# Another order for the head of a convolution and maxout kernel: 38 tiny matmuls for the band, blocks 0 and 1 mixed

## The chip, the core and the metric

The kernel runs on one core of a Trainium2 chip. The engines are TensorE (PE, matmuls; weight loads are shown apart as PEld), VectorE (DVE), ScalarE (ACT), GpSimd (POOL) and SyncE (SP, which only issues transfers here). Each works through its own instructions in order; they wait for each other with semaphores. The metric is the device time of one execution in microseconds; lower is better. Before the change the median of 11 runs is 482.29 us (481.16 to 484.39).

## The reference

x is 8 sequences of 4160 positions of 192 numbers. A causal convolution of 7 taps mixes each position with the six before it; the taps are a softmax over `weight`, one row per head, and a head is 24 neighbouring channels. What comes out is 33280 tokens of 192, and each goes through a maxout layer: three products of 192 by 768, of which the largest element is kept, and one product back to 192.

```python
w = softmax(weight)                                  # 8 heads x 7 taps
y[s, h*24:h*24+24] = sum(w[h, k] * x[s - 6 + k, h*24:h*24+24] for k in range(7))
hid = np.maximum(np.maximum(y @ w1, y @ w2), y @ w3)  # 33280 x 768
out = hid @ w_out                                    # 33280 x 192
```

## The kernel before

The tokens are cut into 65 blocks of 512 (the last is made of the 8 sequence ends). The kernel holds to the order in which it is written: each engine does its instructions as they stand in the code.

*The maxout.* max(a, b, c) is c + max(0, ...) in a form for which only differences are needed: `wd` holds w1 - w3 in partitions 0 to 63 and w2 - w3 in partitions 64 to 127 (`make_wd`, L252), so `copy_w3` (L256) first puts w3 beside w2. `l1(t, j)` (L374) computes the j-th of six groups of 128 hidden units of block t, the "product" of this document: two halves of TensorE (`lp` and `lq`, three passes each) read `yd`, the block after the convolution, which therefore lies twice, in partitions 0 to 63 and 64 to 127. ScalarE takes the relu of `lp` (L387), VectorE the maximum of that and `lq` (L388). `lp` and `lq` come from pools of two PSUM buffers each (`psp`, `psq`), so a product needs the buffers of the one two before it. `st2(t, u)` (L390) is a sixth of the second layer of block t; it also multiplies `yd` with `m16`, the product of w3 and w_out, which carries the part c. `make_m` (L296) makes m16 from `w3t` (w3 transposed by `transpose_w3`, L278) and `wo`.

*The convolution* is a matmul with a band matrix: `band` holds, for each head, the taps along a diagonal, 32 columns and 6 more at a time. It is built at the start (L211 to L268): the exponentials of the taps, spread over 128 partitions by a matmul, seven shifted copies made by VectorE (`shifted`), summed by seven matmuls with an identity (`band_sum`), and four ScalarE copies into place. From block 2 on, `conv(t)` (L312) convolves each head in 32 columns of TensorE, `evac` copies the two PSUM tiles to `ys`, `repack` (L359) moves six pieces by DMA, issued by SP and POOL in turn, into channel order in `yd`, and `double` (L369), a DMA of SP, copies the lower half of `yd` to the upper. Blocks 0 and 1 don't take this way: `conv_dense` (L331) computes all 192 channels dense, in three PSUM banks, each with the 64 channels in both halves, 120 matmuls a block, and evicts them straight into `yd`; the input for it is `xz` (`cast_dense`, L154).

*Inputs.* SP issues x0, the weights, x1, w_out and x2 to x5 one behind the other; ScalarE issues the taps and a part of w2. `cast_x` (L138) is POOL's.

*The head before.* The dense convolution of block 0, products (0,0) to (0,3), the transposes, the dense convolution of block 1, conv 2, products (0,4) and (0,5) with the m products and conv 3 around them. Then the loop (L493): for each t a product of block t and a sixth of the second layer of block t-1 by turns, with the convolutions of later blocks (three blocks ahead, two at a time in even t) after the first product.

*The end.* Block 63's output is one store of POOL; block 64's goes out in four, by SP and ScalarE.

`keep_warm` puts in matmuls on zeros.

Of the kernel before, what the change touches and what calls it, by code (L numbers as in the profile page):

```python
# [14 lines left out]
P = 128  # L15
# [12 lines left out]
def kernel(  # L28
# [58 lines left out]
    xfp = ctx.enter_context(tc.tile_pool(name="xfp", bufs=6))  # L87
# [11 lines left out]
    NDENSE, AHEAD = 2, 3  # L99
# [11 lines left out]
    def load_x(t):  # L111
# [9 lines left out]
        while i < n:  # L121
# [8 lines left out]
            nc.sync.dma_start(out=xf[0:rlen, i:k + 1, :], in_=src)  # L130
# [23 lines left out]
    def cast_dense(t, copies):  # L154
        xf, _, parts = xin[t]
        for v, copy in enumerate(copies):
            for s in range(CYC // 32):
                cut = GRP * (32 * s // GRP + 1)
                a, b = (32 * s, cut) if v == 0 else (cut, 32 * s + 32)
                for (rl, q0, q1) in parts:  # L160
                    copy(  # L161
                        out=xz[t][0:rl, q0:q1, v, :].rearrange("p q (k c) -> p q k c", c=CYC)[:, :, :, a:b],
                        in_=xf[0:rl, q0:q1, :].rearrange("p q (k c) -> p q k c", c=CYC)[:, :, :, a:b])


    ws = const.tile([P, NC, DFF], FP32)
    w3s = const.tile([P, NC, DFF], FP32)
    wos = const.tile([P, NJ, D], FP32)

    def load_w(eng, st, lo, wsrc, f0, f1):  # L170
        eng.dma_start(out=st[lo:lo + HALF, :, f0:f1],
                      in_=wsrc.rearrange("(c r) f -> r c f", r=HALF)[:, :, f0:f1])

    FA = 2 * P
    wk = const.tile([1, NHEAD * KW], FP32)
    nc.scalar.dma_start(out=wk[:], in_=bass.AP(tensor=weight.tensor, offset=0,
                                               ap=[[0, 1], [1, NHEAD * KW]]))
    load_x(0)
    load_w(nc.scalar, ws, HALF, moe_w2, 0, FA)
    load_w(nc.sync, w3s, 0, moe_w3, 0, FA)  # L180
    load_w(nc.sync, ws, 0, moe_w1, 0, FA)
    load_w(nc.sync, w3s, HALF, moe_w3, FA, DFF)
    load_w(nc.sync, ws, 0, moe_w1, FA, DFF)
    load_w(nc.sync, ws, HALF, moe_w2, FA, DFF)
    load_x(1)
    nc.sync.dma_start(out=wos[:], in_=moe_w_out.rearrange("(j p) c -> p j c", p=P))
    for t in range(2, 6):
        load_x(t)

    idle = const.tile([P, NBLK], FP16)  # L190
    nc.vector.memset(idle[:], 0.0)
    def keep_warm(n):

        ps = psp.tile([P, NBLK], FP32, tag="p", name="idle")
        for _ in range(n):
            nc.tensor.matmul(ps[:], lhsT=idle[:, 0:P], rhs=idle[:], start=True, stop=True)  # L196
# [10 lines left out]

    unit = const.tile([P, 32 + 2 * PAD], FP16)  # L211
    nc.vector.memset(unit[:], 0.0)  # L212
    with nc.allow_low_precision("ones and zeros"):
        nc.vector.reduce_sum(out=unit[:, PAD:PAD + 32],
                             in_=ident[:].rearrange("p (a c) -> p c a", c=32), axis=AXX)
# [3 lines left out]
    ones = const.tile([1, P], FP32)  # L219
    nc.vector.memset(ones[:], 1.0)  # L220
    keep_warm(2)
    wps = psq.tile([P, NHEAD, KW], FP32, tag="q", name="wps")
    nc.tensor.matmul(wps[:].rearrange("p h k -> p (h k)"), lhsT=ones[:], rhs=wk[:],  # L223
                     start=True, stop=True)
    wexp = const.tile([P, NHEAD, KW], FP32)
    nc.scalar.activation(out=wexp[:], in_=wps[:], func=AF.Exp)
    wsum = const.tile([P, NHEAD], FP32)
    nc.vector.reduce_sum(out=wsum[:], in_=wexp[:], axis=AXX)
    wrec = const.tile([P, NHEAD], FP32)
    nc.vector.reciprocal(out=wrec[:], in_=wsum[:])  # L230
    taps = const.tile([P, NHEAD, KW], FP16)
    nc.vector.tensor_mul(out=taps[:], in0=wexp[:],
                         in1=wrec[:].unsqueeze(2).to_broadcast([P, NHEAD, KW]))
    shifted = const.tile([P, KW, NHEAD, WIN], FP16)
    for k in range(KW):
        one = unit[:, k:k + WIN]
        nc.vector.tensor_mul(out=shifted[:, k, :, :],
                       in0=bass.AP(tensor=one.tensor, offset=one.offset,
                                   ap=[list(one.ap[0]), [0, NHEAD], [1, WIN]]),
                       in1=taps[:, :, k:k + 1].to_broadcast([P, NHEAD, WIN]))  # L240

    keep_warm(7)
    ps = psq.tile([P, NHEAD, WIN], FP32, tag="q", name="band_sum")
    for k in range(KW):
        nc.tensor.matmul(ps[:], lhsT=ident16[:], rhs=shifted[:, k, :, :],  # L245
                         start=(k == 0), stop=(k == KW - 1))
    keep_warm(3)
    w3h = const.tile([P, NC, DFF], FP16)
    parts_w3 = ((0, 0, FA), (HALF, FA, DFF))
    wd = const.tile([P, NC, DFF], FP16)  # L250

# [4 lines left out]
    def copy_w3(copy, part):  # L256
        lo, f0, f1 = part
        copy(out=w3s[HALF - lo:P - lo, :, f0:f1], in_=w3s[lo:lo + HALF, :, f0:f1])

    def cast_w3(copy, part):  # L260
        lo, f0, f1 = part
        copy(out=w3h[lo:lo + HALF, :, f0:f1], in_=w3s[lo:lo + HALF, :, f0:f1])

    cast_dense(0, (nc.scalar.copy, nc.scalar.copy))
    copy_w3(nc.scalar.copy, parts_w3[0])
    make_wd(0, 1)
    for a in range(4):
# [279 lines left out]
```

The softmax here doesn't subtract the row's maximum and nothing guards it: scores larger than these inputs give would overflow.

## Time and profile before

| | |
|---|---|
| median of 11 runs | 482.29 us |
| the profiled execution | 481.91 us |
| its span | 479.9 us |
| TensorE busy | 468.1 us, 98% of the span |
| VectorE, ScalarE, POOL busy | 366.0, 327.2, 211.2 us |
| first dense matmul | 10.75 us |
| first matmul of conv 2 | 20.89 us |
| first product of block 2 | 33.25 us |
| last matmul / last output in SBUF | 473.7 / 474.4 us |

Times in the profile count from the start of the span. A line of the timeline has the start, the duration, the engine, the line of the kernel, and the output and inputs; "x3" are several instructions in one line. A line of the chain of waits has a start, a duration and what the chain stood on: the chain is followed back from the last instruction to what released it. "Granted clock" is the share of TensorE's full clock that it was given. A transfer's issue and its landing are told apart: "to landing" is from one to the other.

### The profile page before, as it was taken

What the parts mean: (1) busy time and instruction counts of PE and PEld (TensorE: products, weight loads), DVE (VectorE), ACT (ScalarE), POOL (GpSimd) and SP (SyncE); (2) the same over time, 40 slices, a digit from 0 to 9 for tenths busy, and PEclk for the clock granted to TensorE, in tenths of its full rate; (3) what the DMA queues carried; (4) which work ended last, traced back from release to release, by engine and by line L of the source; (5) the groups of instructions that cost most, each with busy time, mean ns of one, the idle gap of its engine ahead of it and who ended that gap; (6) DMA issues with size and microseconds to landing.
All of it is one profiled execution on the core that took longest, in us unless ns stands there. A gap on an engine that the chain in (4) does not pass through costs nothing.

```text
span 479.9 us, 21944 instructions
## 1 busy us (share of the span) xinstructions
PE 468.1 (98%) x9083; PEld 393.8 (82%) x9083; DVE 366.0 (76%) x609; ACT 327.2 (68%) x608; POOL 211.2 (44%) x341
## 2 busy tenths in 40 slices
PE   7899999999999999999999999999999999999994
PEld 3478888888888888888888888888888888888994
DVE  6667877778787877877787777778777777778774
ACT  5676667666666767666666766676676767667663
POOL 2654534553454455345435543543545354345210
PEclk9899999999999999999999999999999999999998
DMA  8867756665756666566566656666656656644312
GB/s 190 227 186 213 207 150 193 171 187 159 204 170 168 183 191 172 152 203 181 168 180 181 178 154 195 170 190 168 177 157 192 186 169 186 170 125 135 112 44 95
DMA packets 67603, 82.08 MB, mean 171 GB/s; under 512 B 9424, under 2 KB 55760, under 8 KB 67504
## 3 DMA queue, kind: packets, MB, share of 16 engines
q1 hardware_dynamic: 53934, 49.01, 40.7%
q0 software_dynamic: 13216, 31.38, 18.4%
q8 instruction: 71, 1.16, 1.1%
q10 hardware_dynamic: 354, 0.30, 0.2%
q14 instruction: 28, 0.23, 0.1%
HBM read 30.31 MB, written 25.56 MB: 116 GB/s over the span
## 4 chain that ended last, share of the span: by engine, by line
PE 97%; DVE 1%; ACT 1%; issue 0%; POOL 0%; POOLq 0%
PE lp L383 32%; PE po L426 30%; PE lq L383 26%; PE G L322 7%; PE D L342 1%; PE idle L196 1%; PE band_sum L245 0%; ACT band L268 0%; DVE h L388 0%; ACT r L387 0%; DVE xz L216 0%; PE pm L301 0%; PE wps L223 0%; PE pm L305 0%; DVE band L218 0%
## 5 line engine op out<-in xcount | busy, mean ns | idle before, releaser
L388 DVE TENSOR_TENSOR h<-r,lq 128x512 f16<-128x512 f16 x390 | 267.1, 685 | 102.0 <-ACT r L387 102.0
L387 ACT ACTIVATE r<-lp 128x512 f16<-128x512 f32 x390 | 232.7, 597 | 135.2 <-PE lp L383 90.3
L383 PE MATMUL lp<-yd,wd 64*128 64x512 f16 x1170 | 315.6, 377 | 0.1
L383 PE MATMUL lq<-yd,wd 64*128 64x512 f16 x1170 | 315.1, 375 | 0.0
L426 PE MATMUL po<-wo,h 64*128 64x192 f16 x3120 | 231.7, 243 | 0.0
L426 PEld LDWEIGHTS <-h 64*128 64x128 f16 x3120 | 187.5, 94 | 25.4
L383 PEld LDWEIGHTS <-wd 64*128 64x128 f16 x2340 | 164.4, 94 | 20.9 <-issue 1.8
L452 POOL DMA_DIRECT2D out_dram<-o x64 | 50.7, 792 | 245.7 <-DVE o L436 233.6
L366 POOL DMA_DIRECT2D yd<-ys x189 | 95.4, 509 | 2.1 <-ACT ys L353 1.5
L426 PE MATMUL po<-m,yd 64*128 64x192 f16 x780 | 87.2, 243 | 0.0
L436 DVE TENSOR_TENSOR o<-a,po 128x384 f32<-128x384 f32 (+1 forms) x132 | 71.4, 542 | 0.6 <-ACT a L435 0.6
L146 POOL CAST x<-xf 112x960 f16<-112x960 f32 x62 | 61.7, 995 | 2.9 <-DMA xf<-in_x_dram 2.8
L435 ACT COPY a<-po 128x384 f32<-128x384 f32 (+1 forms) x132 | 61.7, 469 | 1.2 <-PE po L426 1.2
L426 PEld LDWEIGHTS <-yd 64*128 64x128 f16 x780 | 55.2, 94 | 7.9
L322 PEld LDWEIGHTS <-x 112*32 112x32 f16 x2480 | 29.9, 97 | 13.3 <-issue 13.2
L353 DVE CAST ys<-G 128x512 f16<-128x512 f32 x60 | 38.5, 683 | 0.0
L353 ACT CAST ys<-G 128x512 f16<-128x512 f32 x66 | 35.8, 589 | 2.1 <-PE G L322 0.8
L322 PE MATMUL G<-band,x 112*32 112x103 f16 (+1 forms) x2480 | 34.9, 210 | 0.0
L161 POOL CAST xz<-xf 112x240 f16<-112x240 f32 (+2 forms) x6 | 2.4, 438 | 11.0 <-DMA xf<-in_x_dram 11.0
L196 PE MATMUL idle<-idle 128*128 128x512 f16 x14 | 5.9, 561 | 1.2 <-DVE unit L212 1.2
L342 PE MATMUL D<-band,xz 112*32 112x103 f16 (+1 forms) x240 | 3.8, 230 | 0.9 <-ACT band L268 0.9
L342 PEld LDWEIGHTS <-xz 112*32 112x32 f16 x240 | 3.5, 108 | 1.3 <-issue 1.3
(50 smaller groups left out, 41.2 us busy)
## 6 DMA issues: line engine op xcount, KB each, us to landing
out_dram<-o POOLq DMA_DIRECT2D x64, 384.0 KB, 4.2
xf<-in_x_dram SPq DMA_DIRECT2D x57, 420.0 KB, 4.5
yd<-yd SPq DMA_DIRECT2D x63, 192.0 KB, 3.5
yd<-ys SPq DMA_DIRECT2D x63, 48.0 KB, 3.8
yd<-ys POOLq DMA_DIRECT2D x63, 48.0 KB, 3.3
xf<-in_x_dram SPq DMA_DIRECT2D x8, 252.0 KB, 3.3
yd<-ys SPq DMA_DIRECT2D x63, 32.0 KB, 3.3
yd<-ys POOLq DMA_DIRECT2D x63, 32.0 KB, 3.4
```

What stands on the lines that cost most here:

```text
L146: nc.gpsimd.tensor_copy(out=v[0:rl, q0:q1, :], in_=xf[0:rl, q0:q1, :])
L322: nc.tensor.matmul(G[i][32 * g:32 * g + 32, lo:hi], lhsT=x16[0:rlen, cb:cb + 32], rhs=band[0:rlen, h, cc:cc + hi - lo], start=True, stop=T ...
L342: nc.tensor.matmul(ps[32 * g:32 * g + 32, lo:hi], lhsT=xz[t][0:rlen, q, v, 32 * s:32 * s + 32], rhs=band[0:rlen, h, cc:cc + hi - lo], star ...
L353: copy(out=slots[t][:, i, :], in_=convs[t][i][:])
L366: (nc.sync, nc.gpsimd)[n % 2].dma_start(out=yd[r0:r0 + rows, c, :], in_=slots[t][s0:s0 + rows, half, :])
L383: nc.tensor.matmul(ps[i][:, 0:N], lhsT=wd[row, c, P * j:P * (j + 1)], rhs=y[row, c, 0:N], start=(c == 0), stop=(c == NC - 1))
L387: nc.scalar.activation(out=r[:, 0:N], in_=ps[0][:, 0:N], func=AF.Relu)
L388: nc.vector.tensor_max(out=hs[t][:, j, 0:N], in0=r[:, 0:N], in1=ps[1][:, 0:N])
L426: nc.tensor.matmul(ps[b0, i][:, s % 2, :], lhsT=a, rhs=b, start=first, stop=last)
L435: nc.scalar.copy(out=a[:, ss, :], in_=ps[s0, 0][:, ss, :])
L436: nc.vector.tensor_add(out=outs[t][:, s0:s + 1, :], in0=a[:, ss, :], in1=ps[s0, 1][:, ss, :])
L452: qs[i].dma_start(out=bass.AP(tensor=out.tensor, offset=r * D, ap=[[D, n], [step * D, s1 - s0], [1, D]]), in_=ob[p0:p0 + n, s0:s1, :])
```

## The change

The band is built on 8 partitions: taps of a head in one line each, and 38 matmuls, one for each column of the band window, take a shifted piece of that line (8 by 32) against an 8 by 8 identity. The four ScalarE copies into `band` remain. Block 0's casts go from ScalarE to VectorE.

The dense convolution of blocks 0 and 1 computes each channel once, in two PSUM banks (128 channels and 64), 60 matmuls a block; what is evicted lies in one half of `yd`, and VectorE copies it across to the other (`cross`).

Weights are loaded in three parts of 256 hidden units, x1 after the first; w_out, x2 and x3 are issued by ScalarE, between its relus. POOL casts w3, ScalarE evicts all transposes, which now take their PSUM from `psw`.

The head's order is new: products of block 0 and block 1 by turns, then the second layers of both, with conv 2 and conv 3 in between, both in `psp` and `psq`. Block 2 then runs with no second layer beside it, and the convolutions 4 to 6 are placed anew; from block 4 on the loop is the same, but that x is loaded one block later, into five buffers instead of six. Block 0's second layer adds the m products last. Block 63's output is stored in two parts by SP.

```diff
-    xfp = ctx.enter_context(tc.tile_pool(name="xfp", bufs=6))
+    xfp = ctx.enter_context(tc.tile_pool(name="xfp", bufs=5))
...
+    PW = 2 * P
+    def load_w(part):
+        f = slice(PW * part, PW * (part + 1))
+        for st, lo, wsrc in ((w3s, 0, moe_w3), (ws, 0, moe_w1), (ws, HALF, moe_w2)):
+            nc.sync.dma_start(out=st[lo:lo + HALF, :, f],
+                              in_=wsrc.rearrange("(c r) f -> r c f", r=HALF)[:, :, f])
+    wk = const.tile([NHEAD, KW], FP32)
+    nc.scalar.dma_start(out=wk[:], in_=weight)
     load_x(0)
-    load_w(nc.scalar, ws, HALF, moe_w2, 0, FA)
...
+    load_w(0)
     load_x(1)
-    nc.sync.dma_start(out=wos[:], in_=moe_w_out.rearrange("(j p) c -> p j c", p=P))
-    for t in range(2, 6):
-        load_x(t)
+    load_w(1)
+    load_w(2)
...
+    line = const.tile([NHEAD, WIN + 31], FP16)
...
+    keep_warm(6)
+    nc.scalar.activation(out=wexp[:], in_=wk[:], func=AF.Exp, accum_out=wsum[:])
     nc.vector.reciprocal(out=wrec[:], in_=wsum[:])
+    nc.vector.tensor_scalar(out=line[:, 31:31 + KW], in0=wexp[:], scalar1=wrec[:], scalar2=None,
+                            op0=mybir.AluOpType.mult)
+    bps = psq.tile([32, WIN, NHEAD], FP32, tag="q", name="band_cols")
+    for c in range(WIN):
+        nc.tensor.matmul(bps[:, c, :], lhsT=line[:, WIN - 1 - c:WIN + 31 - c],
+                         rhs=ident16[0:NHEAD, 0:NHEAD], start=True, stop=True)
+    keep_warm(4)
+    for a in range(4):
+        nc.scalar.copy(out=band[32 * a:32 * a + 32, :, 32 * a:32 * a + WIN],
+                       in_=bps[:].rearrange("p c h -> p h c"))
+    cast_dense(0, (nc.vector.tensor_copy, nc.vector.tensor_copy))
...
-    for k in range(KW):
-        nc.tensor.matmul(ps[:], lhsT=ident16[:], rhs=shifted[:, k, :, :],
-                         start=(k == 0), stop=(k == KW - 1))
...
+        for n, slots_ in enumerate((range(4), range(4, 6))):
...
+                    for g, s in enumerate(slots_):
...
+            if n == 0:
+                copies[0](out=yd[0:HALF, 0, :], in_=ps[0:HALF, :])
+                copies[1](out=yd[HALF:P, 1, :], in_=ps[HALF:P, :])
+            else:
+                copies[2](out=yd[0:HALF, 2, :], in_=ps[0:HALF, :])
+
+    def cross(t):
+        yd = dense[t]
+        for c in range(NC):
+            a, b = (slice(HALF, P), slice(0, HALF))[::-1 if c == 1 else 1]
+            nc.vector.tensor_copy(out=yd[a, c, :], in_=yd[b, c, :])
...
+    copy_w3(nc.vector.tensor_copy, 0)
+    make_wd(0, 2)
+    conv_dense(0, (nc.scalar.copy, nc.scalar.copy, nc.scalar.copy))
+    cross(0)
+    cast_w3(0)
+    cast_dense(1, (nc.gpsimd.tensor_copy, nc.scalar.copy))
+    cast_w3(1)
+    cast_w3(2)
+    l1(0, 0)
+    nc.scalar.dma_start(out=wos[:], in_=moe_w_out.rearrange("(j p) c -> p j c", p=P))
+    transpose_w3(0)
+    l1(0, 1)
+    load_x(2, nc.scalar)
+    copy_w3(nc.scalar.copy, 1)
+    conv_dense(1, (nc.scalar.copy, nc.vector.tensor_copy, nc.scalar.copy))
+    cross(1)
+    make_wd(2, 4)
+    l1(1, 0)
+    l1(1, 1)
+    copy_w3(nc.scalar.copy, 2)
+    l1(0, 2)
+    transpose_w3(1)
+    l1(0, 3)
+    load_x(3, nc.scalar)
+    nc.gpsimd.tensor_copy(out=wo[:], in_=wos[:])
+    cast_x(2)
+    make_wd(4, 6)
+    l1(1, 2)
+    l1(1, 3)
+    l1(0, 4)
+    transpose_w3(2)
+    l1(0, 5)
+    make_m(0)
+    make_m(1)
+    l1(1, 4)
+    st2(0, 0, NJ)
+    conv(2, PQ)
+    evac(2, 0)
+    evac(2, 1, nc.vector.tensor_copy)
+    repack(2)
+    load_x(4)
+    load_x(5)
+    st2(0, 1, NJ)
+    l1(1, 5)
+    st2(0, 2, NJ)
+    st2(0, 3, NJ)
+    double(2)
+    cast_x(3)
+    conv(3, PQ)
+    evac(3, 0)
+    evac(3, 1, nc.vector.tensor_copy)
+    repack(3)
+    st2(0, 4, NJ)
+    st2(0, 5, NJ)
+    store(0, 0, 4, (nc.gpsimd,))
+    for u in range(NJ):
+        st2(1, u, NJ)
+    cast_x(4)
+    cast_x(5)
+    load_x(6)
+    double(3)
+    store(1, 0, 4, (nc.gpsimd,))
+    loads_at = {2: (7,), 3: (8, 9)}
+    casts_at = {2: (), 3: (7, 8)}
+    convs_at = {2: (4, 5), 3: (6,)}
+    repacks_at = {2: (4,), 3: (5, 6)}
+    doubles_at = {2: (), 3: (4,), 4: (5, 6)}
+    for t in range(2, NB):
+        for u in loads_at.get(t, (t + 6,)):
+            load_x(u)
+        for u in casts_at.get(t, (t + 5,)):
+            cast_x(u)
+        for u in doubles_at.get(t, (t + 2,)):
+            double(u)
         begin(t)
         l1(t, 0)
...
+            if t == NB - 1 and j == 3:
+                store(t - 1, 0, 2, (nc.sync,))
+        if t == NB - 1:
+            store(t - 1, 2, 4, (nc.sync,))
```

## The prediction

> **What bounds the kernel now.** I read the page first (busy times, slices, chain), then the chain of waits and the timeline of the first 42 us, then the granted clock in windows of one us. From the page:
>
> ```profile
> span 479.9 us, 21944 instructions
> PE 468.1 (98%) x9083; PEld 393.8 (82%) x9083; DVE 366.0 (76%) x609; ACT 327.2 (68%) x608; POOL 211.2 (44%) x341
> PE   7899999999999999999999999999999999999994
> PE 97%; DVE 1%; ACT 1%; issue 0%; POOL 0%; POOLq 0%
> ```
>
> TensorE is full in all slices but the first two and the last. From about 26 us on, a step of the loop is one first-layer product and a sixth of a second layer: the next product starts 1.06 us after the last, with no gap (timeline, TensorE):
>
> ```profile
> 29.01 0.38 PE L383 MATMUL lp<-yd,wd 64*128 64x512 f16 x1
> 29.65 0.58 PE L426 MATMUL po<-wo,h 64*128 64x192 f16 x10
> 30.07 0.38 PE L383 MATMUL lp<-yd,wd 64*128 64x512 f16 x1
> ```
>
> So a product costs TensorE 0.64 us (29.01 to 29.65) and a sixth 0.42 (29.65 to 30.07). The change leaves the loop from block 4 on as it is. It can win or lose only in the head and in the last microseconds, and the question is when the same work is behind TensorE. The chain of waits of the head:
>
> ```profile
> 10.75 1.55 PE D L342 x110
> ...
> 13.40 0.59 ACT r L387
> ...
> 14.02 0.70 DVE h L388
> ...
> 14.73 0.37 PE lp L383
> ```
>
> This is the row that matters most. A product with no second layer beside it ends in relu 0.59, then the maximum 0.70, and only then are its two PSUM buffers free for the next but one. A pair of bare products takes 0.43 + 0.38 + 0.59 + 0.70 + hand-overs = 2.2 us, of which TensorE works 1.28. And the head's clock, in windows (last columns: granted clock, DMA share, GB/s):
>
> ```profile
> 16.00:17.00 1.00, 0.26 (x3) 0.00 (x0) 0.50 (x2) 0.97 (x3) 1.00 (x4) 1.00 1.12 298
> 17.00:18.00 1.00, 0.33 (x6) 0.21 (x6) 1.00 (x2) 0.28 (x1) 1.00 (x2) 1.00 1.09 284
> ...
> 20.00:21.00 1.00, 1.00 (x60) 1.00 (x56) 0.69 (x1) 0.17 (x1) 0.52 (x2) 0.50 1.07 285
> 21.00:22.00 1.00, 1.00 (x50) 0.85 (x40) 0.00 (x0) 0.66 (x2) 0.67 (x2) 0.50 0.29 78
> ```
>
> TensorE was busy 0.26 and 0.33 for two windows; then it ran at half clock from 19.8 to about 23.2.
>
> **The change part by part.** I lay the new orders of the engines out with these durations and look for the time at which the second layer of block 2 starts. Before, that is 41.48 us (its first matmul in the timeline, after block 3's first product at 40.83); both kernels have done the same by then, but for the smaller dense convolutions.
>
> *Band.* wk had landed by 3.42, when the wps matmul's releaser ended. Exp 0.22 and its accumulated sum, 0.35 in all; reciprocal 0.20 and multiply 0.22 with hand-overs: 4.2 us. Then 38 tiny matmuls. No row shows one. Lower bound 13 ns (120 dense matmuls in 1.55 us, four side by side, which these are not); upper 67 ns (12 transposes of 64x64 in 0.80 us). I take 55 ns (the other group, 6 in 0.33 us), as they too are small and each loads its own weights: 2.1 us, and 0.2 drain: 6.5. Four band copies at 0.41: 8.2, against 10.75. The four idle matmuls hide beside them, and so do the six casts of block 0 on VectorE (ScalarE's row 1.45 for six, from x0's landing at 5.07). Gain so far 2.5 us; bounds of the tiny matmuls -1.6 and +0.5 on it. The Trainium skill has a lower price: TensorEngine Tiling (Array Packing), Instruction Overhead, gives every matmul about 60 cycles, however few its columns. At the 2.4 GHz of its first page (Trainium Kernel Development and Optimization, NeuronCore Architecture) that is an estimated 1.0 us for the 38, and the sum would be 1.1 us smaller by it; no run here shows it.
>
> *Dense convolution.* Block 0: 10 rounds of four and 10 of two, at 52 ns a round, 1.04 us for 1.55. But two of three evictions went to different engines before; now all three stand on ScalarE (0.58, 0.52 apart), then a crossing copy. A crossing copy's bounds: 0.20 (a sixth of the 64x1536 copy of 1.22) and 0.69 (an eviction of 512 columns); 0.28 taken, nearer to SBUF to SBUF of 16 bit; at 0.69 it adds 1.9 over both blocks. Bank one is done 0.75 after 8.2, the evictions end at 9.6, 10.1, 10.6, the last crossing at 10.95: the third pass of the first product starts there, before at 12.98. The 2.5 has shrunk to 2.0.
>
> *ScalarE's queue.* Behind relu (0,0) at 11.4 stand, in order: w_out's issue 0.52, the transposes' eviction 0.48, relu (0,1) 0.60, x2's issue 0.57, a w3 copy 0.83, and only then block 1's evictions, 14.8 to 15.9. Issues bounded by ScalarE's own two rows (0.52, 0.69) and SP's row of an x load that was stalled, 4.16; I take the short ones, because ScalarE's queue has nothing outstanding then. TensorE has done block 1's convolution by 13.3 and its next product is block 1's: it stands until 15.7, 2.5 us.
>
> *Mixing.* Ten bare products, two groups of transposes (0.33 each), the two m products (1.25): 8.3 us of TensorE work from 15.7. They go in pairs of 2.2, with two differences wd (1.01 each) and m's copies in VectorE's order between the maxima; (1,4) starts at 25.9, the first sixth of block 0's second layer at 26.5, conv 2 at 26.9. Before, conv 2 was at 20.89: seven products, the m products and a sixth more stand ahead of it now, and make it 6.0 later. The transfers that ScalarE issues are hidden: w_out, issued at 11.9, is wanted at 24.2 and x2, issued at 13.4, at 26.9, and even the landings of before (10.7 and 12.9, behind all the weights) would do. x3, issued at 20.2, lands by 24.7 at the loop's 4.5; at 12.9 it would hold conv 3 by some 2 us.
>
> *Block 2's way.* Conv 2 at 26.9, its evictions end at 28.7 (VectorE's behind a maximum), three issues on SP of 0.62, landing 3.5 (medians 3.3 to 3.8): 33.0. Double: 3.6 (3.5 median): 36.7. Behind that wait stand SP's repack 3 and double 3, which then lands near 42, just ahead of block 3. Beside it TensorE has 6.3 us of work for 9.8 us (conv 2, 3: 1.08; five sixths 2.1; product (1,5) 0.64; block 1's second layer 2.52), so it stands 3.4 us: 1.5 ahead of conv 3, whose cast POOL does after repack 2's issues, and 1.9 ahead of block 2. Before, the double of block 2 was issued at 28.92, landed at 32.5, and its product followed at 33.25 without a gap. Bounds: landings of 2.8 and 3.0 give -1.3, of 4.8 (the head's largest) and 4.5 (x4, x5 are ahead in SP's queue) +2.2.
>
> *Block 2 alone.* Its six products have no second layer beside them, as block 1's is done: conv 4, 5 and products are 4.9 us of work in 6.6. Then block 3's first product, conv 6, and block 2's second layer starts at 44.9: 3.4 after 41.48.
>
> *Clock.* The half-clock stage of before is inside the 41.48. The new head has a pause of 2.5 us and then ten us of TensorE busy a little over half, and may get one of its own, bounded by 0 and three stages; in the one seen, block 1's convolution took 2.14 for 1.55, conv 2 0.86 for 0.57 and product (0,4) 1.24 for 0.64: 1.5 us, less what would have been waits. I add 1.0, one stage. The Trainium skill (TensorE: Matmul & The Clock Gate, Why this matters for your kernels) asks for no pauses over about 3 us, and by that rule nothing is added, as no pause of my layout is so long, and the sum is 1.0 less. The trace of before disagrees: its longest pause ahead of the half clock was 1.3 us.
>
> *End.* Block 63's store goes out in two SP parts, the first some 3 us earlier, instead of one POOL store at 472.81 beside the last four; DMA ran at 364 to 190 GB/s until 476.7. Bounds 0 and -0.5: -0.2. Five xf buffers and loads one block later: a load takes 4.5, its cast comes about 6.5 us after the issue; nothing. If that cover went, POOL would wait and with it repack, which has two blocks of 6.97 us to spare.
>
> Sum: 3.4 + 1.0 - 0.2 = +4.2 us. The profiled execution took 481.91 (span 479.9 and 2.0 around it), so 486.1; it lies 0.38 below the median of 482.29, which gives 486.5.
>
> **The rivals.**
> 1. *Half clock for most of the head.* For it: ten us at half load. Against: the old head, 0.93 busy at 12.8 to 16.2, kept full clock. Three stages instead of one: +2.6, 489.1.
> 2. *ScalarE's issues stall as SP's did.* For: SP's x3 took 4.16. Against: that was with eight loads queued ahead on SP. One stall of 3.6 more ahead of block 1's evictions: 490.1.
> 3. *The other side: bare products don't go in pairs of 2.2.* If the two blocks' products overlap so that relu and maximum never hold TensorE, the 2.5 us of waits in the mixing (10.8 us for 8.3) and 1.7 in block 2 go, and the clock stage with them: 486.5 - 4.2 - 1.0 = 481.3. It decides below about 1.5 us a pair. Against: 13.40, 14.02, 14.73 in the chain, and both blocks draw on the same two buffers a side.
> 4. *The unknown terms all at their lower ends:* landings -1.3, tiny matmuls -1.6, no half clock -1.0: 482.6, no measurable change. For it: the tiny matmuls and the landings at a quiet moment are in no row. Against: all three would have to hold.
>
> **How the numbers follow.** Forecast 0.58 (its own range 484 to 488.5); rivals 1 and 2 0.15 and 0.09; rival 3 0.10; rival 4 0.08. About 0.2% is what a measurement of this kernel tells from no change, 481.3 to 483.3. Faster 0.10, within 0.07, slower 0.83. The range leaves out rival 3, and of rival 2 about half and a little of rival 4: 482.5 to 490.
>
> **What would show it.** Band copies end near 8.2; TensorE idle 2 to 3 us before block 1's first product, released by VectorE's crossing copy; that product near 15.7; conv 2 near 27; TensorE idle before block 2's first product, released by the double's DMA; block 2's second layer near 45; then 6.97 us a block as before. I am wrong if the products of blocks 0 and 1 follow each other in much under 1.1 us, or if block 2 is there before block 1's second layer ends.

## The result, and the profile after

The changed kernel takes 485.75 us (median of 13 runs, 483.99 to 488.17), the kernel before 482.44 beside it (50 runs). The ratio is 1.0066, with a 95% interval of 1.0050 to 1.0082: it is slower by 2.4 to 4.0 us. (A ratio leaves out executions that stand far above the others of their kernel, as three of run e10's do below.) The prediction was 486.5, slower by 4.2. Three of its terms were wrong in size, though, and they happen to cancel, so that it came this close is luck in part: this section and the experiments are about those terms.

The page of the changed kernel:

```profile
span 484.3 us, 21755 instructions
PE 468.2 (97%) x8988; PEld 389.8 (81%) x8988; DVE 366.8 (76%) x610; ACT 324.9 (67%) x605; POOL 211.5 (44%) x340
PE   7777999999999999999999999999999999999996
PE 92%; DMA 3%; ACT 1%; DVE 1%; issue 1%; SPq 1%; ACTq 0%
```

TensorE has the same 468 us of work as before and a span 4.4 us longer. It now reads 7 in four slices (48 us) instead of one, and DMA has 3% of the chain where it had none. The last slice reads 6 instead of 4: the end is better. From there on the steady state is what it was, 13.95 us for two blocks in both traces.

The marks of TensorE's timeline, to be held against the times predicted:

```profile
3.87 1.13 PE L225 MATMUL band_cols<-ident,line 8*32 8x8 f16 x38
...
6.72 1.09 PE L307 MATMUL D<-band,xz 112*32 112x103 f16 x60 [0.76 <-ACT band L229]
...
13.31 0.37 PE L358 MATMUL lp<-yd,wd 64*128 64x512 f16 x1 [1.51 <-ACT yd L313]
...
15.16 0.58 PE L358 MATMUL lp<-yd,wd 64*128 64x512 f16 x1 [0.44 <-DVE yd L323]
...
26.99 0.64 PE L288 MATMUL G<-band,x 112*32 112x103 f16 x40
...
31.24 0.64 PE L288 MATMUL G<-band,x 112*32 112x103 f16 x40 [1.58 <-POOL x L146]
...
38.08 0.43 PE L358 MATMUL lq<-yd,wd 64*128 64x512 f16 x1 [2.56 <-DMA yd<-yd]
...
47.59 0.34 PE L402 MATMUL po<-m,yd 64*128 64x192 f16 x3
```

The 38 tiny matmuls take 1.13 us, 30 ns each, and the first dense matmul starts at 6.72, 4.0 us sooner than before. Block 1's first product comes at 13.31 with its second pass at 15.16, so most of the lead is gone by then; conv 2 starts at 26.99, 6.1 us later than before; block 2's first product waits 2.56 us for the transfer that doubles its rows; and block 2's second layer starts at 47.59, where it was at 41.48. That is a head 6.1 us late, of which the end gives 1.6 back.

The chain of waits across the pause ahead of block 2 (start, duration, what):

```profile
29.59 2.92 DMA yd<-ys
...
32.65 5.39 DMA yd<-yd
```

The doubling transfer, issued at 32.65, landed after 5.4 us. And the granted clock, in windows (the last three columns are granted clock, DMA share and GB/s):

```profile
15.00:16.00 1.00, 0.84 (x6) 0.34 (x7) 0.94 (x3) 0.00 (x0) 0.00 (x0) 0.50 1.12 275
16.00:17.00 1.00, 1.00 (x8) 0.49 (x6) 0.58 (x2) 0.60 (x1) 0.00 (x0) 0.50 1.04 206
...
39.00:40.00 1.00, 1.00 (x37) 0.71 (x40) 0.36 (x1) 0.60 (x1) 0.00 (x0) 0.50 1.13 304
40.00:41.00 1.00, 1.00 (x58) 0.98 (x48) 0.33 (x1) 0.59 (x1) 0.00 (x0) 0.50 0.95 322
```

There are two stages of half clock, 14.4 to 17.8 and 38.3 to 41.7, each behind a pause of TensorE; before there was one, 19.6 to 23.0.

### The profile page after: what moved, and what is told of

The parts are those of the page before. It is cut to its first block, busy times and chain, and to the rows that moved or that the text cites. A ratio compares the mean times of both kernels' runs of the same rounds, so it can differ in the third digit from the quotient of the medians.

```text
span 484.3 us, 21755 instructions
## 1 busy us (share of the span) xinstructions
PE 468.2 (97%) x8988; PEld 389.8 (81%) x8988; DVE 366.8 (76%) x610; ACT 324.9 (67%) x605; POOL 211.5 (44%) x340
## 4 chain that ended last, share of the span: by engine, by line
PE 92%; DMA 3%; ACT 1%; DVE 1%; issue 1%; SPq 1%; ACTq 0%
PE lp L358 31%; PE po L402 29%; PE lq L358 26%; PE G L288 7%; DMA xf<-in_x_dram 1%; DMA yd<-yd 1%; ACT r L362 1%; DMA yd<-ys 1%; DVE h L363 1%; SPq L176 0%; ACT w3s L247 0%; DVE yd L323 0%; SPq L130 0%; ACT w3t L260 0%; DVE yd L314 0%
## 5 line engine op out<-in xcount | busy, mean ns | idle before, releaser
L328 DVE CAST ys<-G 128x512 f16<-128x512 f32 x63 | 40.5, 683 | 2.3 <-PE G L288 2.3
L328 ACT CAST ys<-G 128x512 f16<-128x512 f32 x63 | 34.2, 588 | 4.8 <-PE G L288 3.5
L204 PE MATMUL idle<-idle 128*128 128x512 f16 x10 | 3.8, 530 | 1.2 <-DVE idle L199 1.2
L251 POOL CAST w3h<-w3s 64x768 f16<-64x768 f32 x3 | 2.5, 819 | 4.6 <-DMA w3s<-in_moe_w_dram 4.6
L243 DVE TENSOR_TENSOR wd<-ws,w3s 128x768 f16<-128x768 f32 x3 | 2.9, 956 | 0.9 <-DMA ws<-in_moe_w_dram 0.9
L307 PEld LDWEIGHTS <-xz 112*32 112x32 f16 x120 | 2.0, 96 | 1.6 <-DVE xz L163 1.2
```

What stands on the lines that cost most here:

```text
L328: copy(out=slots[t][:, i, :], in_=convs[t][i][:])
```

## The experiments

All times are set against the kernel before, run beside it on the same chip (482.8 to 482.9 there; the changed kernel's +3.2 us is its 0.66%). Because the steady state never changes, one mark sums up a head: the start of convolutions 9 and 10, in block 6, which is at 61.97 in the trace of before and at 68.09 in the changed kernel's.

| run | edit | median, us | ratio to before (95%) | mark, us |
|---|---|---|---|---|
| e1 | before, split last store | 481.21 | 0.9956 (0.9935 to 0.9978) | 62.53 |
| e2 | after, whole last store | 487.02 | 1.0080 (1.0053 to 1.0106) | 66.78 |
| e3 | after, x4 and x5 loaded early | 483.82 | 1.0016 (0.9995 to 1.0038) | 66.58 |
| e4 | after, idle matmuls in two pauses | 485.23 | 1.0040 (1.0016 to 1.0063) | 67.71 |
| e5 | before, tiny band, split store | 485.24 | 1.0045 (1.0029 to 1.0061) | 67.75 |
| e6 | as e5, dense in two banks | 482.18 | 0.9983 (0.9963 to 1.0002) | 63.69 |
| e7 | as e3, block 5 repacked early | 487.01 | 1.0094 (1.0064 to 1.0124) | 70.93 |
| e8 | as e5, VectorE's copy of w3 later | 484.49 | 1.0038 (1.0018 to 1.0058) | 65.89 |
| e9 | as e8, x4 and x5 loaded late | 481.30 | 0.9964 (0.9939 to 0.9989) | 63.40 |
| e10 | as e3, doublings ahead of loads | 487.58 | 1.0082 (1.0056 to 1.0108) | not read |
| e11 | after, more PSUM for bare products | 484.81 | 1.0048 (1.0024 to 1.0071) | 68.04 |
| e12 | e1, x4 and x5 late, idle matmuls | 480.94 | 0.9955 (0.9935 to 0.9975) | 63.28 |

**The end: e1 and e2.** The same edit, put into the one kernel and taken out of the other.

```
 (e1, into the kernel before; e2 takes the same lines out of the changed one)
             st2(t - 1, j, NJ)
-        store(t - 1, 0, 4, (nc.gpsimd,))
+            if t == NB - 1 and j == 3:
+                store(t - 1, 0, 2, (nc.sync,))
+        if t == NB - 1:
+            store(t - 1, 2, 4, (nc.sync,))
+        else:
+            store(t - 1, 0, 4, (nc.gpsimd,))
```

> The kernel before, with one edit: block 63 is stored as the changed kernel does it, in two parts on SyncE, the first after four of the six sixths, instead of one GpSimd store. Read from the two traces: in the changed kernel the end of the span lies 3.9 us after the last sum is in SBUF, against 5.5 before. Theory A (the store of block 63 alone does this, beside the same last four small stores): 1.6 us faster than before, about 480.8. Theory B (the prediction's price, with 0.5 as its bound): 0.2 faster, 482.2. Theory C (the end gains because the changed kernel's last blocks are otherwise laid out, not by the store): no change, 482.4.

> The changed kernel, with block 63 stored again as one GpSimd store behind its six sixths. Theory A: 1.6 us slower than the changed kernel, 487.3. Theory B: 0.2 slower, 485.9. Theory C: no change, 485.7. Together with the run of the kernel before with the split store this says whether the term of the end stands by itself in both kernels.

In the timeline of e1, its span and VectorE's last sum:

```profile
core 0 of [0], span 479.3 us
...
475.01 0.35 DVE L436 TENSOR_TENSOR o<-a,po 128x192 f32<-128x192 f32 x1 [0.17 <-ACT a L435]
```

and in that of the kernel before:

```profile
core 0 of [0], span 479.9 us
...
474.07 0.35 DVE L436 TENSOR_TENSOR o<-a,po 128x192 f32<-128x192 f32 x1 [0.17 <-ACT a L435]
```

From the end of the last sum to the end of the span it is 3.9 us in e1 (479.3 - 475.36) and 5.5 before (479.9 - 474.42); it is 3.9 in the changed kernel and 5.5 in e2 (484.6 - 479.11). So block 63's store alone is worth 1.6 us at the end, in either kernel: theory A. The times agree for e1 (2.1 us faster, 1.1 to 3.1). In e2 the time moved by 0.7 us (1.0080 against 1.0066, intervals that overlap), which by itself shows neither 1.6 nor nothing. Its profiled head is 1.3 shorter than the changed kernel's, for a reason that the next paragraphs need: it had no second half-clock stage. Which part of the store costs (its size, GpSimd's queue, or the later issue) wasn't separated.

**The doubling's landing: e3.**

```
     load_w(2)
+    load_x(4)
+    load_x(5)
...
     repack(2)
-    load_x(4)
-    load_x(5)
```

> The changed kernel, with the loads of x4 and x5 issued on SyncE right behind the last weights instead of behind the repacking of block 2. In the changed kernel's trace the doubling of block 2, issued at 32.7, landed after 5.4 us, where 3.6 was predicted, and block 2's first product waited for it; TensorE stood 2.6 us, and a stage of half clock followed. Theory A (the two loads, issued just ahead in the same queue, hold the doubling): it lands after about 3.6 us, block 2's first product comes near 36.3 instead of 38.1, the pause shrinks to under 1 us and the second half-clock stage goes with it: 2 to 3.5 us faster than the changed kernel, 482.3 to 483.8. Theory B (the landing of 5.4 has another cause, such as the stores or a slow transfer from SBUF to SBUF): it stays above 5 us and the time within 0.5 us of 485.7. Theory C (the doubling lands sooner, but TensorE then stands for the conv 3 or for VectorE instead): landing near 3.6, time less than 1 us better.

```profile
35.93 0.37 PE L360 MATMUL lq<-yd,wd 64*128 64x512 f16 x1
```

The doubling, issued at 33.25, let block 2's first product read its second half at 35.93, 2.7 us later. The timeline shows no wait ahead of it, where the changed kernel has 2.56. The second half-clock stage was gone and block 2's second layer started at 44.56, 3.0 sooner than in the changed kernel. The time fell by about 2.4 us, from 1.0066 to 1.0016: theory A. But the mark of block 6 is only 1.5 sooner. The chain of e3 shows where the other half went:

```profile
43.96 5.20 DMA xf<-in_x_dram
...
51.28 2.08 DMA yd<-ys
...
53.48 5.95 DMA yd<-yd
```

The doubling of block 5 stands behind late loads and casts and lands after 6 us; TensorE waited 0.9 for it. In the changed kernel the same step is just as late (issued at 53.20, landed after 5.8), but TensorE is not there early enough to wait.

**The half clock: e4, with e2 as a control.**

```
     cross(1)
+    keep_warm(12)
     make_wd(2, 4)
...
     double(3)
+    keep_warm(11)
     store(1, 0, 4, (nc.gpsimd,))
```

> The changed kernel, with idle matmuls in TensorE's two long pauses: 12 of them ahead of block 1's first product (a pause of 12 to 15 us) and 11 ahead of block 2's first product (35.5 to 38.1). They add nothing that anything waits for except TensorE's own order. The changed kernel has two half-clock stages, 14.7 to 17.6 and 38.3 to 41.7. Theory A (the pauses cause the stages, and the stages cost time beyond the waits): both stages go, TensorE's granted clock stays 1.00, and the time falls by 1.5 to 2.5 us, to 483.2 to 484.2. Theory B (a stage hides behind the waits that the bare products have anyway): clock at 1.00, time within 0.5 us of 485.7. Theory C (idle matmuls do not keep the clock, it is the partly filled time after the pauses that loses it): the stages stay, time the same or up to 1 us worse, as the idle matmuls delay what waits behind them.

The clock stayed at 1.00 in every window of the head. The six other traces of this head (the changed kernel, e2, e3, e7, e10, e11) all have a stage that begins between 14 and 17 us, so the idle matmuls do keep the clock, as far as one execution can show it. Conv 2 started at 26.25 instead of 26.99: the first stage costs about 0.7. Of the second stage e2 gives the price, as its code is the changed kernel's up to the last stores. Its windows, behind the same pause of 2.6 us:

```profile
39.00:40.00 1.00, 1.00 (x81) 0.85 (x70) 0.64 (x2) 0.87 (x3) 0.00 (x0) 1.00 1.10 321
40.00:41.00 1.00, 1.00 (x10) 0.52 (x10) 1.00 (x3) 0.79 (x3) 0.53 (x1) 1.00 0.72 253
```

No stage came there, and its mark is 1.3 us sooner (66.78 against 68.09). So the second stage costs 1.3, and whether it comes at all differs from one execution to the next. (The first stage moved as well: in e2 it ran from 16.2 to 19.5.) e4's time, 1.3 us better than the changed kernel's by the ratios (1.0040 against 1.0066, intervals that overlap) and 0.5 by the medians, lies between theories A and B: its block 2 was 2.3 us sooner, but the mark of block 6 only 0.4, with a wait of 1.4 for the doubling of block 5 between them, as in e3.

**What is late next: e7 and e10.** Two attempts to take that last wait away.

```
 (e7, on e3)
-    repacks_at = {2: (4,), 3: (5, 6)}
-    doubles_at = {2: (), 3: (4,), 4: (5, 6)}
+    repacks_at = {2: (4, 5), 3: (6,)}
+    doubles_at = {2: (), 3: (4, 5), 4: (6,)}
 (e10, on e3)
+    double(3)
     load_x(6)
-    double(3)
...
     for t in range(2, NB):
+        for u in doubles_at.get(t, (t + 2,)):
+            double(u)
         for u in loads_at.get(t, (t + 6,)):
             load_x(u)
         for u in casts_at.get(t, (t + 5,)):
             cast_x(u)
-        for u in doubles_at.get(t, (t + 2,)):
-            double(u)
```

> The changed kernel with the loads of x4 and x5 early, as in the run that did this alone, and with block 5's repacking and doubling issued one block sooner (its repacking in block 2, its doubling in block 3). In the run with early loads alone block 2's second layer came 3.0 us sooner, but 1.4 of it was gone again by block 5: TensorE waited 0.9 for a doubling issued at 53.5 that landed after 6 us. Theory A (that wait is what is late next, and the doubling of block 5 was simply issued too late): the 1.4 comes back, 482.3, about 3.4 better than the changed kernel. Theory B (a later load or doubling, of block 4 or 6, takes its place): 483.8 within 0.5, as with early loads alone.

> The changed kernel with the loads of x4 and x5 early, and every doubling put ahead of the same step's loads in SyncE's order. With early loads alone (483.8) the doubling of block 2 landed in 3.0 us, that of block 5, issued right behind a load, in 6, and TensorE waited 0.9 for it; with block 5's repacking sooner as well (487.0) block 4's doubling came 0.2 us behind three loads, landed after 6.3, and TensorE waited 3.2. Theory A (a load issued just ahead in the same queue is what makes a doubling take 6 us): every doubling lands in 3 to 4 us, no wait for one is left in the first 70 us, 482.0 to 482.8. Theory B (doublings are slow whenever any load is under way, whoever is ahead): some still take over 5 us and a wait of about 1 us stays, 483.8 within 0.5.

e7 was a miss: 487.0 (four runs). Its chain:

```profile
40.29 6.74 DMA xf<-in_x_dram
...
48.35 6.25 DMA yd<-yd
```

The earlier repackings pushed three loads of x to 45.4 to 48.2 in SyncE's queue; block 4's doubling, issued at 48.35 right behind them, landed after 6.3 us and TensorE waited 3.2. (The profiled head was 1.1 us behind e3's at conv 2 already, with half clock from 14.5 to 21.3, so not all of its lateness is the repackings'.) e10 put the doublings ahead of the loads, and in its first 68 us TensorE waited for no doubling; but the loads now stand behind the doublings' own waits, and TensorE waited for casts of x instead, 3.8 us in the head (1.6 of them ahead of conv 3, as in the changed kernel) and 7.7 behind it. Its times scatter from 484.4 to 516.9 us and the profiled execution took 500.2, so only its waits are read here. Theory A of e10 fell as a gain: block 2's doubling, with no load near, landed after 2.5 us, but block 5's, 7 us behind the last issue of a load, took 4.8, with the next doubling 0.9 us behind it. Close behind loads it was 5.4 to 6.6 (the changed kernel, e3, e7, e11). A load just ahead is one cause of a slow doubling, then, and not the only one; and whichever of the two goes first, the other is late.

**The band and the order of the blocks: e5, e6, e8.** e5 brings the band and block 0's casts, as the change has them, into the old order, together with e1's store. e6 adds the dense convolutions in two banks and the crossing copies. What e6 leaves as it was before is the order of blocks 0 and 1, the loads and their parts, the engines of w3's casts and evictions, and the places of the later convolutions. e8 is e5 with one copy moved.

```
 (e6, on e5)
-    conv_dense(0, (nc.scalar, nc.vector, nc.scalar))
+    conv_dense(0, (nc.scalar.copy, nc.vector.tensor_copy, nc.scalar.copy))
+    cross(0)
...
-    conv_dense(1, (nc.scalar, nc.vector, nc.scalar))
+    conv_dense(1, (nc.scalar.copy, nc.vector.tensor_copy, nc.scalar.copy))
+    cross(1)
 (e8, on e5)
-    copy_w3(nc.vector.tensor_copy, parts_w3[1])
...
-    make_wd(2, 4)
     begin(0)
     l1(0, 0)
+    copy_w3(nc.vector.tensor_copy, parts_w3[1])
+    make_wd(2, 4)
     l1(0, 1)
```

> The kernel before, with its own order of blocks 0 and 1, and only two parts of the change: the band from 38 tiny matmuls (block 0's casts on VectorE with it) and block 63's store in two SyncE parts. The split store alone gave 481.2 where before gave 482.9. Theory A (the earlier band is worth what the next waits leave of it): the first dense matmul comes near 6.8 instead of 10.75, but the weights' second part lands at 9.4 and VectorE's copy of it, 1.2 long, stands ahead of its eviction and the differences, so that the head keeps 1 to 2 us: 479.2 to 480.2. Theory B (the weights' landings set the head, and the band was hidden): no gain over the split store, 481.2 within 0.5. Theory C (all four microseconds come through): 477.2.

> As the run with band and split store, and the dense convolutions in two banks with VectorE's crossing copies too, in both blocks: what the change does, without its new order of blocks 0 and 1 and without the moved loads. Two convolutions lose 0.5 us of TensorE work each, and each gains a crossing copy behind its last eviction and two more in VectorE's order. Theory A (the new order of the two blocks is what costs; the pieces gain): within 1 us of the run with band and split store, so 479 to 480.5, and 5 to 6 us ahead of the changed kernel. Theory B (the two banks cost too, by the crossing copies, 0.3 to 0.9 each in the two heads): 1 to 2 us above that run. Theory C (it is not the order): near 485.

> As the run with band and split store, and VectorE's copy of the second part of w3, which waits for a landing at 9.4, moved behind block 0's evictions and first product instead of ahead of them. Theory A (VectorE's order holds block 0's first products): the first product comes near 9 instead of 11.3, the third near 13 and the head gains 0.5 to 1.5 more than that run: 478.2 to 479.5. Theory B (the third product waits for the same copy and its difference in either order): within 0.4 of that run.

e6 took 482.2, e5 485.2. None of the theories for e5 had it 4 us slower than e1. The timeline of e5 has the reason:

```profile
20.81 0.41 PE L303 MATMUL G<-band,x 112*32 112x103 f16 x19 [1.06 <-POOL x L146]
24.67 0.67 PE L303 MATMUL G<-band,x 112*32 112x103 f16 x21 [3.45 <-issue]
```

TensorE stops in the middle of conv 2, after 19 of its 40 matmuls, and waits 3.45 us for nothing that the profile shows; half clock runs from 24.0 to 30.9. e8 stops at the same matmul for 2.85. By the ratios it gained 0.3 us on e5, which is within both intervals (theory B: its third product starts at 14.20 and e5's at 14.21, both behind the same copy and difference). The next paragraph takes up that stop.

e6, with 60 matmuls fewer per dense convolution, does not have it there. It comes out 4.0 us faster than the changed kernel (0.9983 against 1.0066). So the new order, with the loads and engines that go with it, costs about 4 us, and the pieces that e6 has don't: that is theory A's main point. How the 4 us divide is shown in part: e3 has the new order with two of the loads early and is 1.6 us from e6 (1.0016 against 0.9983, intervals that overlap), so the late loads of x4 and x5 are 2.4 of the 4.0. The rest was not taken apart. Theory A's other point missed: e6 was not ahead of e1 but behind it (0.9983 against 0.9956, by intervals that overlap). That isn't the pieces either. At convolutions 5 and 6, in block 2, e6 was still ahead of e1, although its crossing copies, behind VectorE's copy of w3, had held the first product for 2.5 us. It fell back after that (e1's line first, then two of e6):

```profile
34.63 1.10 PE L322 MATMUL G<-band,x 112*32 112x103 f16 x80
...
34.37 1.10 PE L303 MATMUL G<-band,x 112*32 112x103 f16 x80
...
40.95 0.39 PE L373 MATMUL lq<-yd,wd 64*128 64x512 f16 x1 [1.14 <-issue]
```

From there to convolutions 7 and 8 (at 49.74, where e1 has 48.58) it lost 1.4 us, and it has a stop there of the same kind as e5's: 1.14 us for nothing that the profile shows.

**TensorE's own code: e9.**

```
 (on e8)
-    for t in range(2, 6):
+    for t in range(2, 4):
         load_x(t)
...
-    cast_x(4)
-    cast_x(5)
...
+    load_x(4, nc.scalar)
     conv(2)
...
     repack(2)
+    load_x(5)
+    cast_x(4)
...
     repack(3)
+    cast_x(5)
```

> As the run with band, split store and VectorE's copy moved behind the first product (484.5), and the loads of x4 and x5, which all stood in the queue from the start, issued later (x4 by ScalarE behind block 1's convolution, x5 behind block 2's repacking; their casts behind the repackings). In that run and in three others TensorE stood in the same place, after its 351st or 352nd matmul, until 2.6 us after a packet of the queue for instructions, and that packet moved at 21.0 to 22.0, when the head's loads had run dry. Theory A (TensorE waits for its own code, and the code lies behind the loads): the packet comes 2 to 3 us sooner, TensorE goes through conv 2 without its pause of 2.9, the half clock behind it goes too: 480.5 to 482. Theory B (the packet's time is not the loads'): the pause stays within 0.5 us of 24.7, and the time within 1 us of 484.5. Theory C (the pause goes and x4 is late instead): pause ahead of conv 4, 483 to 485.

The same place in e9:

```profile
20.94 0.41 PE L300 MATMUL G<-band,x 112*32 112x103 f16 x19 [1.38 <-POOL x L146]
21.69 0.43 PE L300 MATMUL G<-band,x 112*32 112x103 f16 x21 [0.34 <-issue]
```

The stop shrank to 0.34, and the time fell by 3.2 us to 481.3: theory A. (The half clock behind it did not go, though theory A said so: it ran from 22.7 to 26.2.) The profile shows when a packet of the queue for instructions moves, though not for which engine. Read in stretches of 0.2 us, the traces say:

| run | packet, us | TensorE goes on, us | stop, us |
|---|---|---|---|
| before | 21.0 | 23.66 | 0.42 |
| e1 | 21.6 | 24.21 | 1.23 |
| e5 | 22.0 | 24.67 | 3.45 |
| e8 | 22.0 | 24.67 | 2.85 |
| e9 | 19.2 | 21.69 | 0.34 |
| e12 | 20.2 | 22.70 | 1.79 |

In all six TensorE stops at its 351st or 352nd matmul, and goes on 2.5 to 2.7 us after the packet. That delay, the same wherever the packet comes, is the evidence that TensorE waits for it. e6's stop fits too: it ends 2.6 us after a packet at 38.3. In the four runs with all loads queued at the start, the packet moves when they run dry (the DMA share falls from 1.1 to under 0.6 at 21.0 to 22.0); in e9 the share falls from 1.1 to 0.1 between 18.5 and 20.0. The Trainium skill (Runtime: NRT & Kernel Launch, Instruction fetch mechanics) has each engine's code fetched ahead in blocks of 16 KiB by a queue of its own and calls the cost of a boundary mostly hidden; the packets here do carry 0.02 MB, but the cost was up to 3.45 us. In the kernel before, the clock hid most of this: TensorE was at half clock until 23.0 and reached the spot late. e6, with 120 matmuls fewer ahead, came to its 352nd matmul at 26.5, three us after the packet at 23.4, and passed without a stop.

**A version that beats both: e12.** e1's kernel, with x4 and x5 late as in e9, and six idle matmuls ahead of the transposes, where the kernel before lost its clock.

```
 (on e1 with e9's edit)
+    fill = psw.tile([P, NBLK], FP32, tag="w", name="fill")
+    for _ in range(6):
+        nc.tensor.matmul(fill[:], lhsT=idle[:, 0:P], rhs=idle[:], start=True, stop=True)
     for g in range(NJ // 2):
         transpose_w3(g)
```

> The kernel before, with its own band and order and the split store (481.2 alone), and two things that the runs point to: the loads of x4 and x5 issued later, so that TensorE's code is not behind them, and six idle matmuls between product (0,3) and the transposes, where the kernel before is busy 0.26 and 0.33 of two windows and then runs at half clock. Theory A (both the code and the half clock cost this head its time): clock 1.00 throughout, no pause of TensorE at its 352nd matmul, 1 to 2 us better than the split store alone: 479.2 to 480.2. Theory B (what they free is taken by the next wait, x2's cast or the m products): within 0.5 us of 481.2. Theory C (x4 comes late): slower than 481.7, with TensorE waiting for conv 4's cast.

480.94: theory B. The clock held until 23.7, and conv 2 started at 20.28; but then:

```profile
22.70 0.39 PE L381 MATMUL lp<-yd,wd 64*128 64x512 f16 x1 [1.79 <-issue]
```

Though the DMA engines were quiet from 18 on, the packet moved only at 20.2, when TensorE was at its 307th matmul (in e9 it was at the 316th), and the remaining 45 matmuls took 0.7 us of the 2.5. So a TensorE at full clock can outrun the packet even with quiet queues. What asks for the packet isn't shown: in e6 it moved when TensorE was only at about its 269th. The half clock came after the stop, from 23.7 to 27.1. e1 and e12 both beat the kernel before by 0.45% and can't be told apart.

**The pairs of bare products: e11.**

```
     l1(1, 0)
-    l1(1, 1)
+    l1(1, 1, WW)        # WW: both halves from the second layer's PSUM pool
...
-            l1(t, j)
+            l1(t, j, WW if t == 2 and j in (2, 4) else PQ)
 (and so for l1(0, 3), l1(1, 3), l1(0, 5))
```

> The changed kernel, with five of the bare products of blocks 0 and 1 and two of block 2's five inner ones drawing their PSUM from the four buffers of the second layer, which stand empty at that time, instead of from the two of each side. Theory A (the prediction's: two buffers a side make bare products go in pairs of 2.2 us, relu and maximum holding TensorE): TensorE's waits for VectorE's maximum go, and block 2's second layer starts 1 to 2 us sooner than 47.6; of that the run with early loads gave back 1.4 by block 5, so the time falls by 0.3 to 1.5, to 484.2 to 485.4. Theory B (the waits are set by something else: differences wd, landings, ScalarE's queue): block 2's second layer within 0.4 us of 47.6, time within 0.5 us of 485.7.

The edit changes four products of blocks 0 and 1, where the expectation says five.

```profile
37.96 0.80 PE L358 MATMUL l<-yd,wd 64*128 64x512 f16 x5 [3.14 <-DMA yd<-yd]
38.70 1.10 PE L288 MATMUL G<-band,x 112*32 112x103 f16 x80
39.73 4.38 PE L358 MATMUL l<-yd,wd 64*128 64x512 f16 x36
44.04 0.64 PE L288 MATMUL G<-band,x 112*32 112x103 f16 x40
```

Six products in 4.3 us, 1.4 a pair; in e2, at the same clock, they took 5.7 (39.84 to 45.54). So in block 2 two PSUM buffers a side were what made the pairs of 2.0 to 2.2, and theory A holds. (Ahead of conv 2, where four products were changed, TensorE's waits for the maximum went as well, but waits for `wd`, 0.9, and m, 0.5, took their place: conv 2 came at 26.30 instead of 26.99.) Conv 6 came 3.0 us sooner than in the changed kernel, 1.5 sooner than in e2. And nearly all of it was lost: TensorE waited 5.5 us in all for three doublings, and the mark is where the changed kernel has it, 68.04. The time fell by 0.9 us by the ratios (1.0048 against 1.0066, intervals that overlap).

## Why the prediction was right, and where it was not

In the profiled executions the span grew by 4.4 us: 6.1 in the head, less 1.6 at the end, with 0.1 of rounding. (Their times differ by 3.8 and the medians by 3.3; the account is of the spans.) The prediction's sum was 4.4 in the head (3.4 and 1.0 for the clock) and -0.2.

- **Band.** The step that failed is the 55 ns for a tiny matmul: they took 30. The row that I took it from, transposes of 64x64, was the wrong neighbour. It is 1.0 of the 1.5 us by which the band copies ended early, at 6.67 for 8.2; the rest is the chain ahead of them and the drain. The Trainium skill's estimate of 1.0 us for the 38 (TensorEngine Tiling (Array Packing), Instruction Overhead) was near the 1.13 measured. The third pass of the first product came at 9.58 instead of 10.95.
- **Why that lead brought little.** ScalarE's next work, block 1's casts, waited for x1, which landed at 9.59, and everything behind in its queue started from there. Block 1's first product was at 13.31, held at its second pass until 15.16 by the crossing copies, which took 1.52 us instead of the 0.84 of the estimate; 15.7 was predicted. ScalarE's three DMA issues took 0.42, 0.35 and 0.33 us, shorter even than the 0.52 and 0.57 taken, so rival 2 was out.
- **Mixing.** Conv 2 at 26.99 for 26.9 predicted, but with 0.7 of half clock in it that stood elsewhere in the sum; without it 26.25 (e4). From block 1's products to conv 2 it was 11.1 us in e4 (15.13 to 26.25), 11.2 predicted. That relu and maximum hold the pairs is shown by e11 for block 2; in the mixing the same edit brought 0.7 of the 2.5 us of waits that the prediction put there.
- **Block 2's way.** Repacking was as laid out (doubling issued at 32.65, predicted 33.0), but its landing took 5.39, not the 3.6 of the median: mis-sized by 1.8. The prediction named the two loads ahead of it in SyncE's queue as its upper bound, 4.5 us, and took the median all the same, and even that bound was short. e3 shows that they are the cause here: without them ahead it was at most 2.7. Conv 3's wait was 1.58 for 1.5 predicted. From block 2's first product to its second layer it is 9.5 us, 8.2 predicted, and the 1.3 between them is the second half-clock stage.
- **Clock.** One stage at 1.0 was taken; there were two, 0.7 and 1.3. In e2, with the same head, there was one. Rival 1's three were not reached; its 2.6 for two stages more doesn't follow from 1.0 a stage.
- **End.** -1.6 instead of -0.2, and beyond the bound of -0.5: the bound looked only at the transfer rate until 476.7, not at the time from the last sum to the end of the span.

Block 2's second layer was forecast for 44.9, with 1.0 for the clock on top, and came at 47.59. So the head was off by +1.7 (-0.4 for the issue, +1.8 landing, +1.3 second stage, -1.0 taken for the clock, as the first stage's 0.7 is inside the issue's time) and the end by -1.4: these two nearly cancel, and that they do is luck. Rival 3, the faster case, is judged by e11: its condition, pairs under 1.5 us, can be made to hold in block 2, and the time is still 484.8 and not 481.3. Its price was wrong, because it let the products go ahead without asking whether block 2 and later blocks would be there in time.

What costs is the mixed order with the loads as it places them: it puts conv 2 and all that hangs on it 6 us later, and block 2 then waits on a chain of transfers, two late loads ahead of it, with nothing left for TensorE to do. With the old order and loads, and the band, the two banks and the last store of the change, the kernel stands at 482.2 (e6); with the old order and the last store alone, at 481.2 (e1).

## What to carry to other kernels

A head is a row of limits close behind one another: each part that was made faster here (band, loads, PSUM, clock) met the next wait after 1 to 3 us, so a gain has to be followed to the first mark behind which nothing changes, not to the next instruction. Work that a later block hangs on by a long chain of transfers should be started before independent work, however well that fills the engine. And a transfer on a critical path is to be priced by what stands just ahead of it in its queue, not by the median of its kind.

## What the hardware showed that I had not expected

- TensorE can stop, by all signs for its own code. In six traces it stopped at the same matmul, the 351st or 352nd, for 0.3 to 3.45 us, until 2.5 to 2.7 us after a packet of the instruction queue; with the head's loads queued ahead, that packet came when they ran dry. Later stops of e5, e6 and e9 (0.71, 1.14 and 0.48 us) end 2.4 to 2.6 us after a packet too. The profile names such a wait only "issue".
- A transfer from SBUF to SBUF of 192 KB, block 2's doubling, took 2.5 us in e10 and 2.7 in e7 with no load just ahead of it, and doublings took 5.4 to 6.6 close behind loads on the same queue (the changed kernel, e3, e7, e11). The queue isn't the whole of it: one took 4.3 in the kernel before, 0.6 us behind loads, and one 4.8 in e10 with no load near.
- The clock halved behind a pause of 2.56 us in the changed kernel, and stayed whole behind one of 2.61 in e2 and one of 3.14 in e11. The Trainium skill's rule against gaps of over about 3 us (TensorE: Matmul & The Clock Gate, Why this matters for your kernels) did not separate these cases, nor the 1.3 us pause of the kernel before.
- At a granted clock of 1.00 in every window, the first 60 dense matmuls took 1.09 us in the changed kernel and 1.90 in e2, e6 and e11. So the clock that the profile shows doesn't show every slow stretch; the cause is open.
- Three crossing copies took 0.93 us in block 0 and 1.52 in block 1. In block 1 a GpSimd cast ran from 14.14 to 14.96 beside them:

```profile
13.90 1.52 DVE L323 COPY yd<-yd 64x512 f16<-64x512 f16 x3
...
14.14 0.82 POOL L251 CAST w3h<-w3s 64x768 f16<-64x768 f32 x1 [2.81 <-DMA w3s<-in_moe_w_dram]
```

  The other traces, where a GpSimd cast falls elsewhere, bear out that it is the cast. Block 1's three copies took 0.92 us where no cast ran beside them (e4, e7, e11), 0.98 with 0.2 us of overlap (e3), 1.11 with 0.3 (e10), 1.27 with 0.5 (e6) and 1.56 with 0.8 (e2). The casts kept their time (0.82, and 0.99 for the other cast, of x, in e6). The Trainium skill (SBUF — State Buffer, Who interferes with whom) says that the two engines can lock each other out of a shared port, and these rows agree.
